# Second layer: another plan of ticks for the routing, and a token gather by digits of 64 and 20

## The chip, the cores and the metric

The kernel runs on one core of a Trainium2 chip. The metric is the device time of one execution in microseconds. The median of three runs before the change is 1599.07 us (1598.33 to 1605.1).

## The reference

The program has three parts: a spectral mixing of x (4 x 2496 tokens of 256 features), a mixture-of-experts layer with the best expert for each token, and a second such layer in which each of the eight experts takes at most N/8 = 1248 tokens. Only the second layer is touched:

```python
cap = N // E
logits = x @ w_gate
order = np.argsort(-logits.flatten())
assigned = -np.ones(N, dtype=np.int64)
counts = np.zeros(E, dtype=np.int64)
for idx in order:
    tok, e = int(idx) // E, int(idx) % E
    if assigned[tok] >= 0 or counts[e] >= cap:
        continue
    assigned[tok] = e
    counts[e] += 1
for e in range(E):
    mask = assigned == e
    h = np.maximum(x[mask] @ w1[e], 0.0)
    out[mask] = h @ w2[e]
```

## The kernel before

`Route2` replaces the greedy loop by eight phases. A phase finds the expert that fills up next, the tokens that it takes, and a list of their rows; `Moe2` then computes that expert on 1248 tokens in three blocks (384, 384 and 480; in the last phase 512, 384 and 352). The 9984 tokens and the padding of the first layer lie in 128 partitions x 92 columns (`NCOL`).

In a phase five passes search a threshold. Each compares all values with 16 bounds (`cmp`, in two halves, VectorE, tile `q_cmp`), counts by expert (`count`, 12 bf16 matmuls that load `q_cmp` as weights and stream 64 columns of `q_oh`), takes the diagonal (`diag`, tiles `q_dx`, `q_dd`), sums it (`total`, two matmuls) and narrows the bounds (`narrow`, tiles `q_nr`, `q_nn`, `q_th`). Then `pick` and `above` find the full expert and the tokens over its threshold, `left` and `number` update what room is left (`q_f`, `q_qi`), `before` is a prefix count over the partitions in f32 (`q_s`), `close` shuts the expert in the logits (`l<-l,q_pe`), `best0` to `best3` find the best open expert of every token (`q_vr`, `q_g`, `q_fi`, `q_oh`), and `take` marks the tokens (`q_tk`, `q_free`).

For the list, `members` ranks the tokens of the expert and `digits` (`q_base`, `q_ri`, `q_lo`, `q_hb`) splits a rank into a high digit (10 values) and a low digit (128 values). `high` makes a one-hot `q_hh` of the high digit, once times the column number (VectorE) and once times the partition number (ScalarE). `low(i)` makes the one-hot `q_lu` of the low digit for a quarter of 23 columns: 128 x 23 elements, the column index innermost. `gather(i)` runs 23 matmuls for a quarter: the weights are the 128 low-digit columns of one token column (a stride of 23 elements), and 2 x 10 columns of `q_hh` are streamed. The result is 128 x 20 for each quarter, in one PSUM bank (`q_bank`). `index` adds the four quarters and makes the row numbers (`q_ix`), by which GpSimd gathers the tokens from memory with indirect DMAs (tile `y`).

In `Moe2` a block's tokens are transposed (`yt`, TensorE), split into two parts (`yh` by ScalarE, `yl` by VectorE), multiplied by w1 (`e<-yh,w1H` and so on, three matmuls for each product), passed through a relu that splits again (`zh` by ScalarE, `zl` by VectorE) and multiplied by w2. Three PSUM buffers serve both the transposes and the first product. The weights are split by ScalarE (`w1H`, `w2H`) and GpSimd (`w1L`, `w2L`).

All instructions of one engine run in the order in which they are issued. The order is a plan of ticks: `tk.at(k, kind, fn)` puts a function at tick k, and in each tick the kinds run in a fixed order, of which these matter here: loads, `pm` (also inside the first product of a tick), `ev` (relu and token splits), `rt` (routing on VectorE), `pe` (gemms and transposes), `ev2` (weight splits), `pd` (rest of the first layer), `pr` (routing on TensorE). The tables `FAST0`, `PACE1`, `PACE` and `FAST` hold the offsets in ticks of each step for phase 0, phase 1, phases 2 to 6 and phase 7. A block has a gemm of the first product every second tick; the first gemm is at tick 26 for phase 0's expert, at 88 for phase 1's, at 138 for phase 2's and 48 ticks later for each further one. The rest of the first layer (six slots, `g<-w2z,z`) fills TensorE in ticks 1 to 17.

Of the kernel before, what the change touches and what calls it, by code (L numbers as in the profile page):

```python
# [24 lines left out]
P = 128  # L25
# [568 lines left out]
class Setup:  # L594
# [35 lines left out]

    def make3(self, nc, cp):
        io = self.misc[:, 0:128]
        self.iota10 = cp.tile([P, NB2, NCOL], BF16, name="iota10")
        nc.scalar.add(
            self.iota10, io[:, 0:NB2].unsqueeze(2).broadcast_to([P, NB2, NCOL]), 1.0
        )
        self.iota = cp.tile([P, P, 23], BF16, name="iota23")
        nc.scalar.add(self.iota, io.unsqueeze(2).broadcast_to([P, P, 23]), 1.0)

    def make(self, nc):  # L640
        misc = self.misc
# [574 lines left out]
class Moe1:  # L1216
# [341 lines left out]
    "gather": (7, 8, 9, 10), "index": 11,  # L1558
}
FAST0 = {  # L1560
    "cmp": 0, "count": 0, "diag": 1, "total": 1, "pass": 2, "pick": 0, "above": 0, "left": 0,
    "number": 0, "sure": 6, "close": 6, "before": 0, "best0": 6, "take": 1, "best1": 6, "best2": 6,
    "best3": 7, "next": 7, "list": 0, "before2": 1, "digits": 2, "high": 2, "low": 2, "step": 1,
    "gather": (2, 3, 4, 5), "index": 6,
}
PACE = {
    "cmp": 1, "count": 3, "diag": 4, "total": 5.5, "pass": 8, "pick": 0, "above": 0, "left": 1,
    "number": 3, "sure": 9, "close": 2, "before": 2.0, "best0": 3, "take": 4, "best1": 5,
    "best2": 5, "best3": 8, "next": 8, "list": 6, "before2": 4, "digits": 5, "high": 10, "low": 14,
    "step": 2.5, "gather": (15, 17, 20, 22), "index": 23,  # L1570
}
PACE1 = {
    "cmp": 0, "count": 3.5, "diag": 4, "total": 5.5, "pass": 6, "pick": 0, "above": 0, "left": 1,
    "number": 2, "sure": 9, "close": 4, "before": 2.5, "best0": 5, "take": 6, "best1": 7,
    "best2": 7, "best3": 8, "next": 10, "list": 6, "before2": 4, "digits": 5, "high": 10, "low": 13,
    "step": 2.5, "gather": (15, 17, 20, 22), "index": 23,
}
LEAD = {
    "y": 11, "yt": 7, "relu": 2, "g2": 9, "st": 18, "w1l": 24, "w2l": 12, "w1": 19, "w1s": 3,
# [11 lines left out]
class Route2:  # L1591
# [11 lines left out]
    def __init__(self, tc, S, l2, valid, cp, ep):  # L1603
        self.tc, self.S, self.l2, self.valid = tc, S, l2, valid
        t = lambda shape, nm, dt=F32: cp.tile(shape, dt, name=nm)
        self.free = t([P, NCOL], "q_free")
        self.asn = t([P, NCOL], "q_asn")
        self.kk = t([P, E], "q_kk")
        self.l0 = t([P, 1], "q_l0")
        self.bad = t([P, 1], "q_bad")  # L1610
        self.l2c = t([P, E, NCOL], "q_l2c")
        self.lo = self.hi = None
        self.exact = False
        self.turn = {}
# [4 lines left out]
        self.vr, self.g, self.fn, self.on = self.own  # L1619

    def open(self, tmp, pp):
        self.tmp = tmp
# [33 lines left out]
    PLACES = {"cnt": (0, 64), "tot": (128, 128), "bf": (384, 2)}  # L1656
    ACC = 388

    def ps(self, nm, shape):

# [54 lines left out]
    def close(self, pe):  # L1715
        self.tc.eng.vector.tensor_tensor(
            self.l2, self.l2, pe.unsqueeze(2).broadcast_to([P, E, NCOL]), ALU.add
        )

    def best(self, n, s=None):  # L1720

        vec = self.tc.eng.vector
        sh = [P, E, NCOL]
        new = s is None
        if new:
            s = slice(0, NCOL)
# [12 lines left out]
        if n == 0:  # L1739
            vec.tensor_reduce(vr, self.l2[:, :, s].rearrange("p e c -> p c e"), AX.X, ALU.max)  # L1740
        elif n == 1:
            vec.tensor_tensor(
                g, self.l2[:, :, s], vr.unsqueeze(1).broadcast_to(sh), ALU.is_ge
            )
        elif n == 2:
            vec.tensor_tensor(g, g, self.S.w8b[:, :, s], ALU.mult)
            vec.tensor_reduce(fn, g.rearrange("p e c -> p c e"), AX.X, ALU.max)
        else:
            vec.tensor_tensor(on, g, fn.unsqueeze(1).broadcast_to(sh), ALU.is_equal)

# [12 lines left out]
    def phase(self, tk, k, ph, soon):  # L1763
# [233 lines left out]
        def digits():  # L1997
            base = T([P, 1], "q_base")
            vec.tensor_scalar_add(base, st["p"], -1.0)
            ri = T([P, NCOL], "q_ri", I32)  # L2000
            vec.tensor_scalar(ri, st["s"], base, None, ALU.add)
            hi = T([P, NCOL], "q_hi2", I32)
            li = T([P, NCOL], "q_li", I32)
            vec.tensor_single_scalar(li, ri, P - 1, ALU.bitwise_and)
            vec.tensor_single_scalar(hi, ri, 7, ALU.arith_shift_right)
            lo = T([P, NCOL], "q_lo", BF16)
            vec.scalar_tensor_tensor(lo, li, 1.0, st["m"], ALU.add, ALU.mult)
            hb = T([P, NCOL], "q_hb", BF16)
            vec.tensor_scalar_add(hb, hi, 1.0)
            st["lo"], st["hb"] = lo, hb  # L2010

        def high():
            hh = self.late.tile([P, 2, NB2, NCOL], BF16, name=f"q_hh{self.n}", tag="q_hh", bufs=1)
            sh = [P, NB2, NCOL]
            vec.tensor_tensor(
                hh[:, 0], st["hb"].unsqueeze(1).broadcast_to(sh), S.iota10, ALU.is_equal
            )
            vec.tensor_tensor(
                hh[:, 1], hh[:, 0], S.colv.unsqueeze(1).broadcast_to(sh), ALU.mult
            )  # L2020
            nc.scalar.mul(hh[:, 0], hh[:, 0], S.pv)
            st["hh"] = hh

        def low(i):
            self.uniq()
            u = self.late.tile([P, P, 23], BF16, name=f"q_lu{self.n}", tag="q_lu", bufs=4)
            vec.tensor_tensor(
                u,
                S.iota,
                st["lo"][:, 23 * i : 23 * i + 23].unsqueeze(1).broadcast_to([P, P, 23]),  # L2030
                ALU.is_equal,
            )
            st["u", i] = u

        def gather(i):

            o = self.ACC + 2 * NB2 * i
            u = st.pop(("u", i))
            for c in range(23):
                nc.tensor.matmul(  # L2040
                    self.bank[:, o : o + 2 * NB2],
                    u[:, :, c],
                    st["hh"][:, :, :, 23 * i + c].rearrange("p v b -> p (v b)"),
                    start=c == 0,
                    stop=c == 22,
                )

        def index():
            a = T([P, 2, NB2], "q_ia")
            vec.tensor_reduce(  # L2050
                a.rearrange("p v b -> p (v b)"),
                self.bank[:, self.ACC : self.ACC + 8 * NB2].rearrange("p (i x) -> p x i", i=4),
                AX.X,
                ALU.add,
            )
            f = T([P, NB2], "q_if")
# [10 lines left out]
        def pe(t, fn):  # L2067
            tk.at(int(t), "pm" if t % 1 else "pr", fn)
# [8 lines left out]
        else:  # L2077
            for i in range(passes):
                f = FAST if k < soon else c
                tk.at(k, "rt", lambda: cmp(0))  # L2080
                tk.at(k + f["cmp"], "rt", lambda: cmp(1))
                pe(k + f["count"], count)
                tk.at(k + f["diag"], "rt", diag)
                pe(k + f["total"], total)
                k += f["pass"]
                tk.at(k, "rt", narrow)
            for nm, f in (
                ("pick", pick),
# [17 lines left out]
        tk.at(k + c["digits"], "rt", digits)  # L2106
        tk.at(k + c["high"], "rt", high)
        for i in range(4):
            tk.at(k + c["low"] + int(c["step"] * i), "rt", lambda i=i: low(i))
            pe(k + c["gather"][i], lambda i=i: gather(i))  # L2110
        tk.at(k + c["index"], "rt", index)
        return kn, kq, k + c["index"] + 1, st

# [328 lines left out]
```

## Time and profile before

| | |
|---|---|
| median of three runs | 1599.07 us (1598.33 to 1605.1) |
| profiled execution | 1602.92 us, of which span 1601.1 us |
| TensorE matmul busy | 1470.2 us (92%) |
| TensorE weight load busy | 1358.2 us (85%) |
| VectorE busy | 1086.1 us (68%) |
| ScalarE busy | 726.7 us (45%) |
| GpSimd busy | 776.3 us (48%) |
| mean granted TensorE clock | 0.959 |

The span runs from the first to the last instruction. Matmuls overlap and their ends are modelled, so a step between two starts is a better cost than the busy time of one. The chain of work that ended last gives 28% of the span to TensorE and 13% to VectorE, most in pieces of some microseconds that alternate between them. The second layer's routing starts at about 911 us; its last index is made at 1470 us.

### The profile page before, as it was taken

The numbers are of one execution on the slowest core, as the hardware profiler recorded it, in microseconds if no ns is written. First come the engines' busy times: TensorE is split into PE (matmuls) and PEld (weight loads), VectorE is DVE, ScalarE is ACT, GpSimd is POOL, SyncE is SP. The second block draws the span as 40 slices with busy tenths as digits, with TensorE's granted clock in tenths as the row PEclk, the third lists the DMA queues.
The fourth block names the chain that finished last, engine by engine and source line by source line (L and its number), as shares of the span: only waits on it lengthen the run. The fifth ranks groups of instructions, "written<-read, shape, count | busy, mean of one in ns | idle before, by whom it ended". The sixth has DMA issues, their size and how long they took to land. (4 is left out here: it accounts for less than half of the span.)

```text
span 1601.1 us, 32607 instructions
## 1 busy us (share of the span) xinstructions
PE 1470.2 (92%) x11619; PEld 1358.2 (85%) x11619; DVE 1086.1 (68%) x2040; ACT 726.7 (45%) x1557; POOL 776.3 (48%) x759
## 2 busy tenths in 40 slices
PE   6899999798899999999999896898989899999997
PEld 3899999567899998898898775887889888889997
DVE  4797768836997666566566676788596868675321
ACT  4355555555566656566666422222232323233332
POOL 2342323116777776777776204263444444455542
PEclk8899999989999999999999997999999999999999
DMA  7766754763111551221221242212021212122111
GB/s 236 243 211 204 230 158 130 245 197 116 34 38 50 141 145 44 69 60 50 66 59 47 89 122 83 77 36 83 27 92 31 89 31 88 31 82 81 59 43 35
DMA packets 128623, 158.30 MB, mean 99 GB/s; under 512 B 31163, under 2 KB 108206, under 8 KB 128445
## 3 DMA queue, kind: packets, MB, share of 16 engines
q1 hardware_dynamic: 99837, 102.42, 21.1%
q0 software_dynamic: 15744, 36.23, 7.5%
q10 hardware_dynamic: 12864, 17.41, 3.3%
q8 instruction: 96, 1.57, 0.4%
q14 instruction: 82, 0.67, 0.1%
HBM read 170.69 MB, written 53.30 MB: 140 GB/s over the span
## 5 line engine op out<-in xcount | busy, mean ns | idle before, releaser
L145 DVE TENSOR_TENSOR w1l<-w1r,w1h 128x512 fp32r<-128x512 f32 x168 | 209.3, 1246 | 83.5 <-ACT w1h L145 70.1
L145 PE MATMUL g<-w2h,hl 128*128 128x264 f32 x1152 | 240.7, 290 | 8.6 <-DVE hl L145 8.2
L145 POOL TENSOR_TENSOR w2l<-w2r,w2h 128x528 fp32r<-128x528 f32 x144 | 197.9, 1393 | 96.9 <-ACT w2h L145 36.5
L145 ACT ACTIVATE zh<-e 128x384 fp32r<-128x384 f32 (+3 forms) x192 | 99.4, 518 | 317.2 <-PE e L145 302.2
L145 DVE SCALAR_TENSOR_TENSOR zl<-e,zh 128x384 fp32r<-128x384 f32 (+3 forms) x192 | 112.4, 586 | 129.7 <-ACT zh L145 110.0
L145 PEld LDWEIGHTS g<-w2h,hl 128*128 128x128 f32 x1152 | 188.9, 189 | 11.2 <-DVE hl L145 10.6
L145 PE MATMUL g<-mh,w1h 128*128 128x256 f32 x672 | 193.5, 288 | 2.8 <-issue 2.8
L145 PE MATMUL g<-ml,w1h 128*128 128x256 f32 x672 | 191.9, 286 | 4.2 <-issue 3.9
L145 PE MATMUL g<-mh,w1l 128*128 128x256 f32 x672 | 191.8, 285 | 3.2 <-issue 3.2
L145 PE MATMUL e<-w2H,zh 128*128 128x256 f32 (+1 forms) x640 | 187.3, 293 | 0.0
L145 PE MATMUL e<-w2H,zl 128*128 128x256 f32 (+1 forms) x640 | 182.3, 285 | 0.0
L145 PE MATMUL e<-w2L,zh 128*128 128x256 f32 (+1 forms) x640 | 182.0, 284 | 0.0
L145 PE MATMUL g<-w2l,hl 128*128 128x264 f32 x576 | 164.5, 286 | 0.0
L145 POOL DMA_INDIRECT out_dram<-o,yi x80 | 86.8, 1085 | 154.8 <-ACT o L145 139.6
L145 PE MATMUL e<-yh,w1H 128*128 128x384 f32 (+3 forms) x384 | 146.2, 381 | 14.0 <-DVE zl L145 8.0
L145 PE MATMUL e<-yl,w1H 128*128 128x384 f32 (+3 forms) x384 | 138.4, 360 | 0.0
L145 PE MATMUL e<-yh,w1L 128*128 128x384 f32 (+3 forms) x384 | 138.3, 360 | 0.0
L145 PEld LDWEIGHTS g<-mh,w1h 128*128 128x128 f32 x672 | 130.4, 194 | 9.0 <-issue 5.7
L145 PEld LDWEIGHTS g<-ml,w1h 128*128 128x128 f32 x672 | 130.2, 194 | 5.8 <-issue 5.0
L145 PEld LDWEIGHTS g<-mh,w1l 128*128 128x128 f32 x672 | 130.3, 194 | 4.5 <-issue 4.5
L145 ACT CAST w2h<-w2r 128x528 fp32r<-128x528 f32 x144 | 93.1, 646 | 84.7 <-PE g L145 43.4
L145 PEld LDWEIGHTS e<-w2H,zh 128*128 128x128 f32 (+1 forms) x640 | 122.4, 191 | 1.5
(1219 smaller groups left out, 3941.9 us busy)
## 6 DMA issues: line engine op xcount, KB each, us to landing
w1r<-in_moe_w_dram SPq DMA_DIRECT2D x168, 256.0 KB
w2r<-in_moe_w_dram SPq DMA_DIRECT2D x144, 256.0 KB
x_d<-row ACTq DMA_DIRECT2D x36, 257.0 KB
a<-a_d SPq DMA_DIRECT2D x36, 256.0 KB
w2x<-in_moe_w_dram SPq DMA_DIRECT2D x16, 512.0 KB
w1s<-in_moe_w_dram SPq DMA_DIRECT2D x32, 256.0 KB
w2s<-in_moe_w_dram SPq DMA_DIRECT2D x32, 256.0 KB
xt<-in_x_dram SPq DMA_DIRECT2D x16, 468.0 KB
```

The costliest lines, as they stand in the source:

```text
L145: r = f(*args, **kw)
```

## The change

The gather is turned: the low digit has 64 values and the high digit 20. `low(i)` writes 23 x 64 with the digit innermost, so that a token column's 64 values are contiguous. `high` makes two tiles of 20 x 92, and eight short steps `turn(i, v)` on ScalarE copy them quarter by quarter to 23 x 2 x 20, the first of them scaled by the partition number. In `gather(i)` the 40 high-digit columns are the weights and the 64 low-digit columns are streamed; the result is 40 x 64 for each quarter. `gathered` adds the quarters, two f32 matmuls (`turned`) turn the sum back to 128 x 20, and `index` reads that from PSUM. The large iota of 128 x 23 becomes 64 values.

The two reductions over the eight experts (`best0`, `best2`) become trees of three maxima. The tables change: in `PACE` `close` and `best0` come two ticks later, `best1` one, `best2` two, `digits` three, `index` one; a new entry `wait` puts the first pass's count later, and in phase 1 it puts off a pass that falls within three ticks of the first gemm's tick less three. `index` of phase 0 comes one tick later, and so does its first gemm (tick 27); the later ones keep their ticks (88, 138, ...). Phases 2 to 6 start one tick earlier.

```diff
 PACE = {
-    "cmp": 1, "count": 3, "diag": 4, "total": 5.5, "pass": 8, "pick": 0, "above": 0, "left": 1,
-    "number": 3, "sure": 9, "close": 2, "before": 2.0, "best0": 3, "take": 4, "best1": 5,
-    "best2": 5, "best3": 8, "next": 8, "list": 6, "before2": 4, "digits": 5, "high": 10, "low": 14,
-    "step": 2.5, "gather": (15, 17, 20, 22), "index": 23,
+    "wait": 1, "cmp": 1, "count": 3, "diag": 4, "total": 5.5, "pass": 8, "pick": 0, "above": 0, "left": 1,
+    "number": 3, "sure": 9, "close": 4, "before": 2.0, "best0": 5, "take": 4, "best1": 6,
+    "best2": 7, "best3": 8, "next": 8, "list": 6, "before2": 4, "digits": 8, "high": 10, "low": 14,
+    "step": 2.5, "gather": (15, 17, 20, 22), "index": 24,
 }
...
+    def tree(self, o, x, dt):
+        n = x.shape[2]
+        for h in (4, 2, 1):
+            y = o.unsqueeze(1)
+            if h > 1:
+                y = self.half[dt, h][:, :, :n]
+            self.tc.eng.vector.tensor_tensor(y, x[:, 0:h], x[:, h : 2 * h], ALU.max)
+            x = y
...
+        def turn(i, v):
+            if v == 0:
+                st["hh", i] = self.late.tile(
+                    [P, 23, 2, NH], BF16, name=f"q_hh{self.n}_{i}", tag=f"q_hh{i}", bufs=1
+                )
+            o = st["hh", i][:, :, v]
+            x = st["hx"][v][:, :, 23 * i : 23 * i + 23].rearrange("p b c -> p c b")
+            if v == 0:
+                nc.scalar.mul(o, x, S.pv)
+            else:
+                nc.scalar.copy(o, x)
...
         def low(i):
             self.uniq()
-            u = self.late.tile([P, P, 23], BF16, name=f"q_lu{self.n}", tag="q_lu", bufs=4)
+            sh = [P, 23, HALF]
+            u = self.late.tile(sh, BF16, name=f"q_lu{self.n}", tag="q_lu", bufs=4)
             vec.tensor_tensor(
                 u,
-                S.iota,
-                st["lo"][:, 23 * i : 23 * i + 23].unsqueeze(1).broadcast_to([P, P, 23]),
+                S.iotal.unsqueeze(1).broadcast_to(sh),
+                st["lo"][:, 23 * i : 23 * i + 23].unsqueeze(2).broadcast_to(sh),
                 ALU.is_equal,
             )
...
                 nc.tensor.matmul(
-                    self.bank[:, o : o + 2 * NB2],
-                    u[:, :, c],
-                    st["hh"][:, :, :, 23 * i + c].rearrange("p v b -> p (v b)"),
+                    self.bank[: 2 * NH, o : o + HALF],
+                    hh[:, c].rearrange("p v b -> p (v b)"),
+                    u[:, c],
                     start=c == 0,
                     stop=c == 22,
                 )
...
+        def gathered():
+            a = st["a"] = T([2 * NH, HALF], "q_ga")
             vec.tensor_reduce(
...
+        def turned():
+            for h in range(2):
+                nc.tensor.matmul(
+                    self.bank[HALF * h : HALF * h + HALF, self.IDX : self.IDX + NH],
+                    st["a"],
+                    S.ident[: 2 * NH, h : 2 * NH : 2],
+                    start=True,
+                    stop=True,
+                )
...
             for i in range(passes):
                 f = FAST if k < soon else c
-                tk.at(k, "rt", lambda: cmp(0))
+                o = f["wait"] if "wait" in f and (i == 0 or 0 < soon <= k < soon + 3) else 0
+                late = o if f is PACE1 else 0
+                tk.at(k + late, "rt", lambda: cmp(0))
+                tk.at(k + late + f["cmp"], "rt", lambda: cmp(1))
+                pe(k + o + f["count"], count)
...
-            tk.at(k + c["low"] + int(c["step"] * i), "rt", lambda i=i: low(i))
+            t = k + c["low"] + int(c["step"] * i)
+            tk.at(t, "rt", lambda i=i: low(i))
+            for v in range(2):
+                tk.at(max(t - 1 + v, k + c["high"]), "ev2", lambda i=i, v=v: turn(i, v))
             pe(k + c["gather"][i], lambda i=i: gather(i))
+        tk.at(k + c["index"] - 1, "rt", gathered)
+        pe(k + c["index"] - 1, turned)
         tk.at(k + c["index"], "rt", index)
```

## Rows read from the trace of the kernel before

**Rows 1.** Busy time by stretch: TensorE, weight load, VectorE, ScalarE, GpSimd; clock, DMA.

```profile
960.00:990.00 30.00, 17.05 (x135) 13.89 (x133) 18.92 (x41) 4.61 (x10) 10.11 (x11) 0.67 0.34 101
...
1213.00:1292.00 79.00, 73.25 (x575) 67.43 (x574) 60.20 (x145) 23.73 (x53) 36.88 (x39) 0.98 0.19 61
...
1470.00:1601.00 131.00, 121.33 (x859) 117.24 (x857) 35.62 (x70) 43.57 (x100) 56.93 (x69) 0.98 0.15 48
```

**Rows 2.** TensorE's waits from 990 to 1475 us: in total, times, longest.

```profile
PE e L145 <- DVE zl L145: 8.0, 11, 2.1
PE yt L145 <- DVE zl L145: 5.6, 3, 3.9
...
PE e L145 <- DVE q_free L145: 3.6, 2, 1.9
PE q_bank L145 <- DVE q_base L145: 3.4, 2, 1.8
...
PE yt L145 <- DVE q_f L145: 1.4, 3, 0.5
```

**Rows 3.** TensorE in order of time, 1258 to 1278 us: start, duration, instruction.

```profile
1258.20 0.28 PE L145 MATMUL q_bank<-q_s,misc 128*128 128x1 f32 x2
...
1271.71 0.73 PE L145 MATMUL q_bank<-q_oh,q_cmp 128*128 128x64 bf16 x12
1272.28 0.36 PE L145 MATMUL e<-w2H,zh 128*128 128x256 f32 x1
...
1272.71 0.28 PE L145 MATMUL e<-w2H,zh 128*128 128x256 f32 x1
1272.83 0.28 PE L145 MATMUL e<-w2L,zh 128*128 128x256 f32 x1
...
1275.93 1.64 PE L145 MATMUL q_bank<-q_hh,q_lu 128*128 128x20 bf16 x23
1277.42 0.37 PE L145 MATMUL e<-w2H,zh 128*128 128x256 f32 x1
```

**Rows 4.** Weight loads by form: count, busy us, mean ns, idle before.

```profile
L145 PEld LDWEIGHTS <-q_cmp 128*128 128x128 bf16 x385 | 18.3, 102 | 23.5 <-DVE q_cmp L145 10.6 <-issue 7.2 <-DVE q_w L145 3.3
...
L145 PEld LDWEIGHTS <-q_cmp 128*64 128x64 bf16 x35 | 3.8, 109 | 2.0
```

**Rows 5.** VectorE's groups by form.

```profile
L145 DVE TENSOR_TENSOR q_lu<-iota,q_lo 128x2944 bf16<-128x2944 bf16 x32 | 61.0, 1913 | 0.0
...
L145 DVE TENSOR_REDUCE q_vr<-l 128x92 f32<-128x736 f32 x7 | 11.0, 1567 | 0.0
L145 DVE TENSOR_REDUCE q_fi<-q_g 128x92 bf16<-128x736 bf16 x7 | 10.2, 1452 | 0.2
...
L145 DVE TENSOR_TENSOR f_hh<-f_hh,v 117x1540 bf16<-117x1540 bf16 x4 | 7.0, 1749 | 0.0
...
L145 DVE TENSOR_TENSOR l<-l,q_pe 128x736 f32<-128x736 f32 x7 | 6.4, 916 | 0.0
L145 DVE TENSOR_TENSOR q_hh<-q_hh,colv 128x920 bf16<-128x920 bf16 x8 | 5.1, 637 | 0.3
...
L145 DVE TENSOR_TENSOR q_g<-q_g,w8b 128x736 bf16<-128x736 bf16 x7 | 3.8, 542 | 0.2
```

**Rows 6.** VectorE in order of time, `narrow` to `above` of phase 4, first and last.

```profile
1240.36 0.28 DVE L145 TENSOR_REDUCE q_nr<-q_bank 128x16 f32<-128x128 f32 x1
...
1244.94 0.35 DVE L145 TENSOR_TENSOR_SCAN q_s<-ones,q_bi 128x92 f32<-128x92 bf16 x1
```

**Rows 7.** TensorE and VectorE in order of time, 978 to 988 us.

```profile
978.65 0.66 PE L145 MATMUL yt<-ident,y 128*128 128x128 f32 x2 [2.60 <-DMA y<-x_d,q_ix]
...
984.22 2.89 DVE L145 TENSOR_TENSOR q_cmp<-q_v,q_th 128x768 bf16<-128x768 f32 x2
...
987.71 0.67 PE L145 MATMUL e<-yh,w1H 128*128 128x384 f32 x1
```

**Rows 8.** ScalarE's scaling of the one-hot, by form.

```profile
L145 ACT ACTIVATE q_hh<-q_hh,misc 128x920 bf16<-128x920 bf16 x8 | 8.5, 1062 | 15.3 <-DVE q_hh L145 13.6 <-issue 1.7
```

More of the change, by code (lines that the diff above doesn't have):

```diff
@@ L41 @@
 NB2 = 10
+HALF = 64
+NH = 20
 CLOSED = 30000.0
@@ L632, in make3 @@
         io = self.misc[:, 0:128]
[L633 to L638, printed above, removed]
+        self.iotah = cp.tile([P, NH, NCOL], BF16, name="iotah")
+        nc.scalar.add(self.iotah, io[:, 0:NH].unsqueeze(2).broadcast_to([P, NH, NCOL]), 1.0)
+        self.iotal = cp.tile([P, HALF], BF16, name="iotal")
+        nc.scalar.copy(self.iotal, io[:, 1 : 1 + HALF])
     def make(self, nc):
@@ L1557 @@
     "best3": 1, "next": 2, "list": 1, "before2": 2, "digits": 3, "high": 6, "low": 6, "step": 1,
-    "gather": (7, 8, 9, 10), "index": 11,
+    "gather": (7, 8, 9, 10), "index": 12,
 }
@@ L1563 @@
     "best3": 7, "next": 7, "list": 0, "before2": 1, "digits": 2, "high": 2, "low": 2, "step": 1,
-    "gather": (2, 3, 4, 5), "index": 6,
+    "gather": (2, 3, 4, 5), "index": 7,
 }
 PACE = {
-    "cmp": 1, "count": 3, "diag": 4, "total": 5.5, "pass": 8, "pick": 0, "above": 0, "left": 1,
-    "number": 3, "sure": 9, "close": 2, "before": 2.0, "best0": 3, "take": 4, "best1": 5,
-    "best2": 5, "best3": 8, "next": 8, "list": 6, "before2": 4, "digits": 5, "high": 10, "low": 14,
-    "step": 2.5, "gather": (15, 17, 20, 22), "index": 23,
+    "wait": 1, "cmp": 1, "count": 3, "diag": 4, "total": 5.5, "pass": 8, "pick": 0, "above": 0, "left": 1,
+    "number": 3, "sure": 9, "close": 4, "before": 2.0, "best0": 5, "take": 4, "best1": 6,
+    "best2": 7, "best3": 8, "next": 8, "list": 6, "before2": 4, "digits": 8, "high": 10, "low": 14,
+    "step": 2.5, "gather": (15, 17, 20, 22), "index": 24,
 }
 PACE1 = {
-    "cmp": 0, "count": 3.5, "diag": 4, "total": 5.5, "pass": 6, "pick": 0, "above": 0, "left": 1,
+    "wait": 2, "cmp": 0, "count": 3.5, "diag": 4, "total": 5.5, "pass": 6, "pick": 0, "above": 0, "left": 1,
     "number": 2, "sure": 9, "close": 4, "before": 2.5, "best0": 5, "take": 6, "best1": 7,
     "best2": 7, "best3": 8, "next": 10, "list": 6, "before2": 4, "digits": 5, "high": 10, "low": 13,
-    "step": 2.5, "gather": (15, 17, 20, 22), "index": 23,
+    "step": 2.5, "gather": (15, 17, 20, 22), "index": 24,
 }
@@ L1619, in __init__ @@
         self.vr, self.g, self.fn, self.on = self.own
+        self.half = {
+            (d, h): t([P, h, NCOL], f"e_m{i}{h}", d) for i, d in enumerate((F32, BF16)) for h in (4, 2)
+        }
     def open(self, tmp, pp):
@@ L1654, in t @@
         return self.tmp.tile(shape, dt, name=nm + str(self.n), tag=nm, bufs=bufs)
-    PLACES = {"cnt": (0, 64), "tot": (128, 128), "bf": (384, 2)}
-    ACC = 388
+    PLACES = {"cnt": (0, 0), "tot": (64, 0), "bf": (192, 2)}
+    IDX = 196
+    ACC = 216
     def ps(self, nm, shape):
@@ L1739, in best @@
         if n == 0:
-            vec.tensor_reduce(vr, self.l2[:, :, s].rearrange("p e c -> p c e"), AX.X, ALU.max)
+            self.tree(vr, self.l2[:, :, s], F32)
         elif n == 1:
@@ L1746, in best @@
             vec.tensor_tensor(g, g, self.S.w8b[:, :, s], ALU.mult)
-            vec.tensor_reduce(fn, g.rearrange("p e c -> p c e"), AX.X, ALU.max)
+            self.tree(fn, g, BF16)
         else:
@@ L2003, in digits @@
             li = T([P, NCOL], "q_li", I32)
-            vec.tensor_single_scalar(li, ri, P - 1, ALU.bitwise_and)
-            vec.tensor_single_scalar(hi, ri, 7, ALU.arith_shift_right)
+            vec.tensor_single_scalar(li, ri, HALF - 1, ALU.bitwise_and)
+            vec.tensor_single_scalar(hi, ri, 6, ALU.arith_shift_right)
             lo = T([P, NCOL], "q_lo", BF16)
@@ L2012, in high @@
         def high():
[L2013 to L2016, printed above, removed]
-            )
[L2018 to L2022, printed above, removed]
+            sh = [P, NH, NCOL]
+            e, x = (
+                self.late.tile(sh, BF16, name=f"q_h{c}{self.n}", tag=f"q_h{c}", bufs=1) for c in "ex"
+            )
+            vec.tensor_tensor(e, st["hb"].unsqueeze(1).broadcast_to(sh), S.iotah, ALU.is_equal)
+            vec.tensor_tensor(x, e, S.colv.unsqueeze(1).broadcast_to(sh), ALU.mult)
+            st["hx"] = e, x
+        def turn(i, v):
[9 more added lines that the diff above has]
+                nc.scalar.copy(o, x)
         def low(i):
             self.uniq()
-            u = self.late.tile([P, P, 23], BF16, name=f"q_lu{self.n}", tag="q_lu", bufs=4)
+            sh = [P, 23, HALF]
+            u = self.late.tile(sh, BF16, name=f"q_lu{self.n}", tag="q_lu", bufs=4)
             vec.tensor_tensor(
                 u,
-                S.iota,
-                st["lo"][:, 23 * i : 23 * i + 23].unsqueeze(1).broadcast_to([P, P, 23]),
+                S.iotal.unsqueeze(1).broadcast_to(sh),
+                st["lo"][:, 23 * i : 23 * i + 23].unsqueeze(2).broadcast_to(sh),
                 ALU.is_equal,
@@ L2035, in gather @@
         def gather(i):
-            o = self.ACC + 2 * NB2 * i
-            u = st.pop(("u", i))
+            o = self.ACC + HALF * i
+            u, hh = st.pop(("u", i)), st.pop(("hh", i))
             for c in range(23):
                 nc.tensor.matmul(
-                    self.bank[:, o : o + 2 * NB2],
-                    u[:, :, c],
-                    st["hh"][:, :, :, 23 * i + c].rearrange("p v b -> p (v b)"),
+                    self.bank[: 2 * NH, o : o + HALF],
+                    hh[:, c].rearrange("p v b -> p (v b)"),
+                    u[:, c],
                     start=c == 0,
@@ L2046, in gather @@
                 )
-        def index():
-            a = T([P, 2, NB2], "q_ia")
+        def gathered():
+            a = st["a"] = T([2 * NH, HALF], "q_ga")
             vec.tensor_reduce(
-                a.rearrange("p v b -> p (v b)"),
-                self.bank[:, self.ACC : self.ACC + 8 * NB2].rearrange("p (i x) -> p x i", i=4),
+                a,
+                self.bank[: 2 * NH, self.ACC : self.ACC + 4 * HALF].rearrange(
+                    "p (i x) -> p x i", i=4
+                ),
                 AX.X,
@@ L2055, in index @@
             )
+        def turned():
[7 more added lines that the diff above has]
+                )
+        def index():
+            a = self.bank[:, self.IDX : self.IDX + NH].rearrange("p (v b) -> p v b", v=2)
             f = T([P, NB2], "q_if")
@@ L2079, in phase @@
                 f = FAST if k < soon else c
-                tk.at(k, "rt", lambda: cmp(0))
[L2081 to L2085, printed above, removed]
+                o = f["wait"] if "wait" in f and (i == 0 or 0 < soon <= k < soon + 3) else 0
[3 more added lines that the diff above has]
+                pe(k + o + f["count"], count)
+                tk.at(k + o + f["diag"], "rt", diag)
+                pe(k + o + f["total"], total)
+                k += f["pass"] + late
                 tk.at(k, "rt", narrow)
```

## The prediction

> **What bounds the kernel now.** I read the busy shares by stretch first, then the waits of TensorE, then single rows of the engines. In the table by stretch [rows 1] the last 640 us are the second layer. From 1470 us on TensorE alone sets the time: nothing of the routing is left there and it is busy for 121.3 of 131 us, the rest being the gaps that its modelled ends leave and the close of the program. In a steady phase (1213 to 1292) it is busy 73.3 of 79 us, VectorE 60.2 and ScalarE 23.7, so TensorE is the bound there too, with some 6 us of waits. From 960 to 990 it is the other way round: TensorE is busy 17 of 30 us at a granted clock of 0.67, because the first tokens of the layer wait for the routing. The list of TensorE's waits from 990 to 1475 us [rows 2] names VectorE on every line; its 13 lines add up to 38 us, of which the five shown here make 22. So three things can shorten the layer: less TensorE work for the routing, fewer of these 38 us, and a shorter passage at 970 to 988.
>
> **TensorE: the gather.** Each of eight phases has 4 quarters of 23 matmuls. Today one loads 128 strided columns of `q_lu` and streams 20. A quarter begins at 1275.93 and the next work at 1277.42: 1.49 us, 65 ns a pair [rows 3]. Afterwards a pair loads 40 contiguous columns and streams 64. The nearest row is the count, which loads contiguous columns and also streams 64: 12 pairs from 1271.71 to 1272.28, 47.5 ns each [rows 3]. Bounds: 65 ns above (nothing won), and below 30 ns, because 256 streamed columns step by 0.12 us (1272.71 to 1272.83), so 64 of them need 30 [rows 3]. I take 47.5, being nearest in shape: 92 x 17.5 ns = 1.6 us less in a phase. New are the two turning matmuls in f32. One f32 matmul of the prefix count is recorded as two passes of together 0.28 us [rows 3], so two cost 0.56 at most; half of that where their start-up overlaps other work. I take 0.4. Net 1.2 us a phase, and over phases 1 to 7, where TensorE is the bound, **8 us** less (between 3 more and 20 less). Phase 0's share lies in the passage below.
>
> The line by form of the weight loads shows 102 ns for 128 columns of `q_cmp` and 109 ns for its last group of 64 [rows 4]: fewer columns are no shorter load. The Trainium skill ("TensorE: Matmul & The Clock Gate", section "Weight-path perf modes — Fast Weight Load (FWL) and DoubleRow") says that the fast load is on only with 128 weights that are not fp32, at four columns a cycle. That speaks against this part: 40 columns would fall out of it, and load in 40 cycles instead of 32. By its figures that is an estimate of 3 ns a pair, 2 us over seven phases, and the 8 us above would be 6 (the total 1584 instead of 1582). The 64-column row agrees with it in sign.
>
> **VectorE: about the same work.** `low` falls from 2944 to 1472 elements, which looks like half. But its second operand is now one value held over 64 elements. The row that has such an operand, all bf16, is `f_hh<-f_hh,v`: 1540 elements in 1749 ns, whereas `q_lu` does 2944 in 1913 on average [rows 5]. With 736 f32 elements in 916 ns the slope is 1.04 ns an element and the fixed part 153 [rows 5]; so the new `low` costs 1.68 us, four of them 0.9 us less than today. Were it as fast an element as today it would be 1.0 us each, 3.8 us less; that is the other bound. I take 1.68. `high` doubles to 1840 elements twice: from 542 ns at 736 and 637 at 920 [rows 5] the slope is 0.52, so 1.11 us each, 0.95 us more in all. `gathered` reads 256 elements instead of 80, some 0.2 more. The tree in place of the first reduce (1567 ns) is three f32 steps of 368, 184 and 92 elements, 0.54 + 0.34 + 0.25 = 1.13; in place of the second (1452) three bf16 steps, 0.35 + 0.26 + 0.21 = 0.82 [rows 5]. That is 1.1 us less. Sum: 0.9 us less in a phase of 60; 3.7 less with the other bound of `low`, 0.6 less if the bf16 steps run no faster than f32. The amount hardly matters; where it stands does.
>
> **The plan of ticks.** A phase is 48 ticks of 1.65 us. Today `close`, `best0`, `take`, `best1`, `best2`, `members`, the next phase's `first` and its comparisons, and `digits` all sit in ticks 99 to 108 (phase 2), just where a new block's `yl` and `zl` have to pass the same queue. The four large ones shown alone are 4.5 us there (0.92 + 1.57 + 0.54 + 1.45) [rows 5], and they come right behind `narrow`, `pick` and `above`, some 18 instructions in tick 97; in phase 4 they run from 1240.36 to 1245.29, 4.9 us or three ticks [rows 6]. VectorE arrives late in tick 99, and TensorE waits. The waits that carry names from this run are `q_free` 3.6, `q_base` 3.4 and `q_f` 1.4 us [rows 2], and those on `zl` (8.0 and 5.6) partly. Afterwards `close` and `best0` come two ticks later, `best1` apart from `best2`, and `digits` stands at 110, behind the first count; the first comparisons have three ticks instead of two before their count. What goes: `q_base` and `q_f` wholly and most of `q_free`, 7 us, and a third of the 13.6 on `zl`, 4.5. What is late next: `pick` and `above` still are one block of 4.9 us in one tick [rows 6], so the long wait for `zl` behind them (up to 3.9 us) and the `q_s` waits stay. And because VectorE has the same work, some of it moves: `high` at tick 112 now stands for 2.2 us in front of `narrow`. I take **9 us** (0 to 18).
>
> **The passage at 970 to 988.** Today the second pass of phase 1 (`narrow`, both comparisons) is put where the first three token tiles arrive. The transpose starts at 978.65; the comparisons run from 984.22 for 2.89 us, slowed by GpSimd's splits; only behind them come two `yl` and the count, and the first gemm at 987.71 [rows 7]. Afterwards this pass is at ticks 23 and 24 with gemm1 at 27, and the third pass waits until 28. So `narrow` and the comparisons run in the idle 4 us before 979. Against that the index is late by `gathered` and the turn: about 0.8 us, less the 4 x 0.4 us that the quarters win. Count 1 and its total now stand between the transposes on TensorE (about 2 us at the low clock). I get gemm1 at about 985: **3 us** (0 to 5).
>
> **What it adds in waits.** The turn waits on TensorE for `gathered`; queued behind it are the next gemms. One tick lies between the last quarter and it, `gathered` takes 0.4, so 0.3 us a phase, 2 us (0 to 6). On ScalarE eight turns a phase replace one scaling of 920 elements, 1062 ns [rows 8]. A turn has 460: between 0.53 and 1.06, I take 0.65 us, 5.2 in all, 4 more than now. ScalarE is busy 24 of 79 us [rows 1], which hides them; they come one or two a tick. Behind a turn stand `zh` and the weight splits, hence 1 us for late `zh`. The iota for 23 columns also goes from ScalarE, in tick 5, while TensorE works off the first layer's rest: nothing, and nothing if that cover were gone but the copy's own length, once.
>
> **Sum.** 8 + 9 + 3 - 2 - 1 = 17 us. The profiled execution took 1602.9 us (span 1601.1 and 1.8 around it), so it would take 1585.9. The median of the runs is 1599.1, 3.8 below it. Predicted: **1582 us**.
>
> **Rivals.**
> 1. *The waits only move and the gather is no faster.* For it: VectorE's work is the same to 1 us in 60, and every wait is on VectorE. Against it: `close` to `digits` is visibly the dense place. Then 3 us of the passage and a few of the waits are left, less the turn: 1595.
> 2. *More goes than I take.* The gather at 30 ns (20 us), nearly all waits of this stretch (18), the passage (4): some 40 us, 1560. For it: nothing but these rows' bounds; against it, `pick` and `above` are untouched.
> 3. *ScalarE holds up TensorE: slower.* A turn stands in front of `zh` and waits for `high` or for its place; with three PSUM buffers shared by gemm1 and the transposes a late `zh` stops gemm1. It decides once `zh` is later than the two or so ticks that the buffers give. Price, if each turn shows fully: 8 x 0.65 x 7 = 36 us, less the 20 gained: 1615. Against it: ScalarE's low share and the turns' spread; for it: in the first and last phase three turns share the tick of `high`.
> 4. *It doesn't do what it says in one part:* `low` is not cheaper. That is already my forecast; were it to halve, 3 us of VectorE a phase, of which TensorE would see the waits on `q_lu`, 3 us in all: 1579.
>
> **Chances.** Forecast (with 4) 0.58, own range 1574 to 1590; rival 1 0.19; rival 2 0.12; rival 3 0.11. About 0.5% (8 us) is what a measurement of this kernel can tell from no change. Under 1591: nearly all of the forecast, rival 2 and a quarter of rival 1, 0.72. Within: most of rival 1 and a little of the rest, 0.17. Slower: rival 3, 0.11. The range reaches from halfway to rival 2, 1567, to just past rival 1, 1599.
>
> **What would show it.** Right: gathers of 23 pairs in about 1.1 us; `q_lu` at 1.7 us in spite of half the elements; the waits on `q_base` and `q_f` gone; the first gemm of the layer 3 us earlier; the stretch after the last index as long as before. Wrong: gathers still at 1.5 us; new waits of TensorE on `q_hh`, `q_ga` or on `zh` by ScalarE; a steady phase still 79 us long.

## The result, and the profile after

The changed kernel takes **1580.1 us** (median of 6 runs, 1574.8 to 1582.8), the kernel before 1597.7 us (6 runs, 1594.0 to 1605.1): ratio 0.9888, 95% interval 0.9862 to 0.9914, some 18 us. The forecast was 1582. The profiled execution took 1574.8 us (span 1572.8). In it the second layer, from its first transpose (`e_am`) to the end of the span, lasts 665.0 us (907.8 to 1572.8); before it was 684.8 (916.3 to 1601.1): 19.8 us. The first layer's code is the same and its time moves by several us from run to run, so below the second layer stands beside each ratio. Each such time comes from one profiled execution, and here that execution is the shortest of the six.

The table by stretch of the changed kernel: the start of the layer, one steady phase, the part after the last index; its columns are those of [rows 1].

```profile
950.00:980.00 30.00, 20.31 (x169) 15.97 (x167) 23.35 (x57) 10.07 (x19) 12.44 (x13) 0.72 0.35 101
1195.60:1271.20 75.60, 68.82 (x575) 63.42 (x574) 60.04 (x147) 30.14 (x60) 34.58 (x38) 1.00 0.20 63
1442.00:1572.80 130.80, 120.99 (x854) 116.63 (x852) 35.40 (x70) 43.61 (x100) 56.95 (x69) 0.97 0.15 48
```

A steady phase falls from 79.0 to 75.6 us, TensorE in it from 73.3 to 68.8, at a clock of 1.00 instead of 0.98; VectorE keeps its 60 us. The last part is as long as before.

TensorE's waits of the changed kernel, 974 to 1447 us (in total, times, longest), against [rows 2]:

```profile
PE e L147 <- DVE zl L147: 9.9, 5, 3.1
PE yt L147 <- DVE zl L147: 6.0, 2, 3.1
PE q_bank L147 <- DVE q_cmp L147: 5.4, 9, 1.2
PE q_bank L147 <- DVE q_dd L147: 5.4, 8, 1.9
PE q_bank L147 <- DVE q_s L147: 5.3, 2, 3.6
PE q_bank L147 <- DVE q_dx L147: 4.2, 8, 0.7
PE q_bank L147 <- DVE q_bi L147: 3.3, 3, 1.1
...
PE q_bank L147 <- DVE q_lu L147: 0.6, 3, 0.2
PE q_bank L147 <- DVE q_ga L147: 0.5, 1, 0.5
```

`q_free`, `q_base` and `q_f` are gone, as forecast. Yet the sum is not smaller (45 us, before 38): TensorE arrives earlier and waits for other results of the same VectorE, which ends 42.6 of the 45 us.

One quarter of the gather on TensorE, the answer to [rows 3], and the first gemm of the layer, which answers to [rows 7]:

```profile
948.04 0.83 PE L147 MATMUL q_bank<-q_lu,q_hh 128*40 128x64 bf16 x23
948.80 0.92 PE L147 MATMUL g<-w2z,z 128*128 128x256 f32 x3
...
968.99 1.76 DVE L147 TENSOR_TENSOR q_cmp<-q_v,q_th 128x768 bf16<-128x768 f32 x2
...
974.46 0.69 PE L147 MATMUL e<-yh,w1H 128*128 128x384 f32 x1 [0.46 <-ACT yh L147]
```

A quarter takes 0.76 us from start to next start, 33 ns a pair instead of 65. The comparisons of the second pass take 1.76 us instead of 2.89, and the first gemm comes 66.7 us after the layer's first transpose (974.5 - 907.8) instead of 71.4.

VectorE and ScalarE by form (busy us, mean ns, idle before), against [rows 5] and [rows 8]:

```profile
L147 DVE TENSOR_TENSOR q_lu<-iotal,q_lo 128x1472 bf16<-128x1472 bf16 x32 | 54.1, 1698 | 0.0
L147 DVE TENSOR_TENSOR q_he<-q_hb,iotah 128x1840 bf16<-128x1840 bf16 x8 | 8.9, 1118 | 0.2 <-DVE q_hb L147 0.2
...
L147 DVE TENSOR_TENSOR e_m<-l 128x368 f32<-128x368 f32 x7 | 3.7, 531 | 0.0
...
L147 DVE TENSOR_TENSOR q_vr<-e_m 128x92 f32<-128x92 f32 x7 | 3.7, 527 | 0.2
L147 DVE TENSOR_TENSOR e_m<-e_m 128x184 f32<-128x184 f32 x7 | 3.5, 502 | 0.2
L147 DVE TENSOR_REDUCE q_ga<-q_bank 40x64 f32<-40x256 f32 x8 | 3.3, 417 | 9.2 <-PE q_bank L147 9.2
...
L147 ACT ACTIVATE q_hh<-q_he,misc 128x460 bf16<-128x460 bf16 x32 | 36.2, 1130 | 4.6 <-POOL rowz L147 3.1 <-issue 1.5
L147 ACT COPY q_hh<-q_hx 128x460 bf16<-128x460 bf16 x32 | 32.5, 1016 | 0.0
```

### The profile page after: what moved, and what is told of

Same layout as the page of the kernel before. It is cut to its first block, busy times and chain, and to the rows that moved or that the text cites. A ratio compares the mean times of both kernels' runs of the same rounds, so it can differ in the third digit from the quotient of the medians.

```text
span 1572.8 us, 32766 instructions
## 1 busy us (share of the span) xinstructions
PE 1445.6 (92%) x11651; PEld 1330.5 (85%) x11651; DVE 1091.1 (69%) x2076; ACT 778.6 (50%) x1613; POOL 771.1 (49%) x759
## 3 DMA queue, kind: packets, MB, share of 16 engines
q8 instruction: 96, 1.57, 0.4%
## 5 line engine op out<-in xcount | busy, mean ns | idle before, releaser
L147 DVE TENSOR_TENSOR w1l<-w1r,w1h 128x512 fp32r<-128x512 f32 x168 | 216.1, 1287 | 70.9 <-ACT w1h L147 53.7
L147 PE MATMUL g<-mh,w1h 128*128 128x256 f32 x672 | 189.9, 283 | 3.5 <-issue 3.3
L147 PE MATMUL g<-mh,w1l 128*128 128x256 f32 x672 | 188.3, 280 | 1.0 <-issue 1.0
L147 PE MATMUL e<-yh,w1H 128*128 128x384 f32 (+3 forms) x384 | 145.1, 378 | 10.3 <-DVE zl L147 9.9
L147 PEld LDWEIGHTS g<-mh,w1h 128*128 128x128 f32 x672 | 127.1, 189 | 9.6 <-issue 7.1
L147 ACT CAST w2h<-w2r 128x528 fp32r<-128x528 f32 x144 | 93.1, 647 | 75.6 <-PE g L147 48.3
L147 PEld LDWEIGHTS g<-ml,w1h 128*128 128x128 f32 x672 | 127.0, 189 | 4.2 <-issue 3.5
L147 PEld LDWEIGHTS g<-mh,w1l 128*128 128x128 f32 x672 | 126.9, 189 | 3.0 <-issue 3.0
```

The source lines that it names most:

```text
L147: r = f(*args, **kw)
```

## The experiments

The kernel before ran beside the others each time, so ratios are to it. The edits below are shown in short. "Two phases" is the time between two indices two steady phases apart, with TensorE's busy time, the sum of its waits and the mean clock in it.

| run | ratio, 95% | second layer | two phases | busy | waits | clock |
|---|---|---|---|---|---|---|
| before | 1 | 684.8 | 157.9 | 147.6 | 10.3 | 0.97 |
| e1 changed kernel | 0.9882 (0.985 to 0.9913) | 664.1 | 151.2 | 137.6 | 13.7 | 1.00 |
| e2 old gather | 0.992 (0.989 to 0.9951) | 670.1 | 153.1 | 143.0 | 10.1 | 0.99 |
| e3 old plan | 0.9981 (0.996 to 1.0001) | 681.0 | 159.7 | 142.2 | 17.5 | 0.97 |
| e4 old reductions | 0.9885 (0.9853 to 0.9917) | 665.2 | | | | |
| e5 low in pairs | 0.9812 (0.9793 to 0.983) | 655.0 | 147.9 | 138.6 | 9.2 | 0.99 |
| e6 high written directly | 0.9881 (0.9862 to 0.99) | 659.8 | | | | |
| e7 above a tick later | 0.9868 (0.9845 to 0.9891) | 665.5 | | | | |
| e9 spread undone | 0.9963 (0.9941 to 0.9986) | 678.1 | 159.6 | 142.1 | 17.5 | 0.97 |
| e10 waiting ticks undone | 0.9907 (0.9879 to 0.9934) | 668.3 | 153.6 | 139.3 | 14.4 | 0.99 |
| e11 e5 and e6 together | 0.9807 (0.9779 to 0.9835) | 653.5 | 147.9 | 138.6 | 9.3 | 0.99 |
| e12 old plan, low in pairs | 0.9936 (0.9914 to 0.9957) | 670.2 | 152.6 | 139.5 | 13.1 | 0.99 |

The two phases lie early in the layer. The same quantities from the second index of the layer to the last, in which every steady phase lies and the passage at its start doesn't:

| run | time | busy | waits | clock |
|---|---|---|---|---|
| before | 408.4 | 376.5 | 31.9 | 0.96 |
| e1 changed kernel | 391.3 | 354.8 | 36.5 | 0.98 |
| e2 old gather | 397.0 | 367.0 | 30.0 | 0.98 |
| e5 low in pairs | 386.7 | 356.4 | 30.3 | 0.97 |
| e9 spread undone | 407.4 | 362.4 | 45.0 | 0.96 |

**One part undone at a time (e1 to e4).**

> The changed kernel itself, as the level for the three runs beside it. Both theories: 1580 us, about 17 below the kernel before.

Changed kernel again: 1552.6 us against 1572.4, on a chip on which both are shorter; the ratio agrees.

```diff
 e2: make3, PLACES, digits, high, low, gather, index as before; turn, gathered and turned left out
 e3: PACE and PACE1 as before, but  "index": 23  ->  "index": 24  (the turn needs the tick)
     and  g - LEAD0["soon"]  ->  g - LEAD0["soon"] - 1  (the later blocks then come a tick later too)
 e4: -            self.tree(vr, self.l2[:, :, s], F32)
     +            vec.tensor_reduce(vr, self.l2[:, :, s].rearrange("p e c -> p c e"), AX.X, ALU.max)
     (and the same for fn)
```

> The changed kernel with the gather of before (digits of 128 and 10, 128 strided weight columns, no turns), new plan and trees kept; its index still in the new tick. Theory G (the gather's TensorE time is the gain): a pair goes from 33 to 65 ns, 92 pairs and eight phases less the turning matmuls, 20 us slower than the changed kernel, 1598 or a little less. Theory P (the plan of ticks gives half of it, as predicted): 8 slower, 1588.

> The changed kernel with the tables of before for phases 1 to 6 (close, best0 to best2, digits in their old ticks, no wait), all one tick later because the index needs a tick more; new gather and trees kept. Theory P: 9 us of waits and 3 to 4 of the passage come back, 1592. Theory G: only the passage, 4 us, 1584.

> The changed kernel with the two reductions of before in place of the trees: 1.1 us more of VectorE in each of seven phases. If VectorE's length in that stretch goes to TensorE one to one: 7 us slower, 1587. If it lies beside TensorE's work: 1580.

Undoing the gather costs 6.0 us of the second layer, undoing the plan 16.9, the trees 1.1, which can't be told from nothing. Theory P holds for the larger share, and more than it expected; theory G falls. The old gather has 5.4 us more of TensorE in two phases and 3.6 fewer waits; from the second index to the last 12.2 more and 6.5 fewer: more than half of what the fast gather saves comes back as waiting. Taken from the other side, the plan with the trees (e2) is worth 0.8%, 12.6 us, and the gather with the trees (e3) 0.2%, with an interval that still holds 1: without the plan the faster gather buys next to nothing. Two things keep these prices rough. In e3 every later block comes one tick of 1.65 us later than in the changed kernel, and that may be part of its 16.9. And e2 also gives the counts their second place in the PSUM bank back (`PLACES`), which no run takes by itself.

**VectorE's load, ScalarE's turns, the block of pick and above (e5 to e7).**

```diff
 e5: lo holds each value twice, [P, NCOL, 2], and low compares with it in pairs
-  lo[:, 23i:23i+23].unsqueeze(2).broadcast_to([P, 23, HALF])
+  lo[:, 23i:23i+23].unsqueeze(2).broadcast_to([P, 23, HALF // 2, 2])
 e6: VectorE writes the high one-hot as [P, NCOL, 2, NH] (in pairs too); ScalarE only scales, in place
 e7: -"above": 0   +"above": 1   in PACE and PACE1
```

> The changed kernel, with the low digit kept twice beside itself, so that the innermost step of every operand of the comparison is 1 again. A comparison of 1472 elements should go from 1.68 to 0.95 us, 2.9 us less of VectorE in a phase. Theory V (VectorE's load in the stretch of the lows holds TensorE back, and ate most of what the gather saved): 8 to 15 us faster than the changed kernel, second layer 650 to 657 us instead of 665. Theory B (the wait is one block of VectorE, pick and above, and the load elsewhere has cover): within 2 us of it.

> The changed kernel with the high one-hot written by VectorE straight into the layout of the weights (pairs, so that the innermost step is 1), and only four scalings by ScalarE: the eight turns of 1.0 to 1.1 us in a phase become four of about 0.7. If ScalarE's turns hold up zh and so TensorE (rival 3 of the prediction, in a small form): 3 to 10 us faster. If ScalarE's share has cover: within 2 us of the changed kernel.

> The changed kernel with above one tick behind pick in phases 1 to 6, so that zl and yl can pass between the two parts of the block of 4.9 us. Theory B: the waits for zl behind the block (4.3 us in two phases) and the drop of the granted clock that follows a long one go: 6 to 12 us faster. Theory V: 2 us or less.

Theory V holds in its number, the rest falls. In e5 `low` costs 0.92 us in the median (mean 995 ns), as VectorE's row by form shows:

```profile
L147 DVE TENSOR_TENSOR q_lu<-iotal,q_lo 128x1472 bf16<-128x1472 bf16 x32 | 31.6, 995 | 0.0
```

VectorE is busy 111.6 us in two phases instead of 120.2, TensorE's waits fall from 13.7 to 9.2, and the time by 0.7% against the changed kernel. The waits that went, first of e1, then of e5 (`q_dx` and `q_lu` end none there any more), each with the table line of its two phases:

```profile
PE q_bank L147 <- DVE q_dx L147: 2.5, 4, 0.7
...
PE q_bank L147 <- DVE q_dd L147: 2.1, 4, 0.7
PE q_bank L147 <- DVE q_lu L147: 0.4, 2, 0.2
```

```profile
1175.50:1326.70 151.20, 137.58 (x1149) 126.72 (x1148) 120.16 (x294) 60.45 (x120) 69.99 (x76) 1.00 0.20 63
```

```profile
PE q_bank L147 <- DVE q_dd L147: 0.6, 2, 0.3
```

```profile
1190.60:1338.50 147.90, 138.60 (x1149) 127.69 (x1148) 111.55 (x294) 60.49 (x120) 69.09 (x76) 0.99 0.20 65
```

So TensorE does wait on the time that VectorE takes, not only on its places. That this time is `low`'s own is shown in part only: of the 8.6 us, `low` gives 4.8. Another 4.3 are `q_cmp` (13.2 to 11.0) and `q_dd` (5.1 to 3.0), which have the same work as before but run beside a weight split of GpSimd less often; such a meeting stretches them by about 1 us. From the second index to the last `low` gives 16.4 of 21.0. No run parts the two. With four of the eight turns gone and the other four shorter (e6), and with `above` a tick later (e7), the ratios stay within the interval of the changed kernel's.

**The price of a gather pair (e8).** Seven extra groups of 23 matmuls behind the last index, all else as in the changed kernel; n is the number of columns loaded, `near` says whether they are adjacent.

```diff
+  for n, near, cols in (128, no, 20), (128, yes, 20), (128, no, 64), (128, yes, 64),
+                       (40, no, 64), (40, yes, 64), (40, yes, 20):
+      v = pw as "(c n) -> n c" if near else "(n c) -> n c"      # c: 23
+      23 x matmul(bank[:n, :cols], v[:, :, c], pm[:, :cols])
```

> The changed kernel with seven groups of 23 bf16 matmuls added among the last gemms, on a constant tile: weights of 128 or 40 columns, strided by 23 or contiguous, and 20 or 64 streamed columns; its time is longer by their sum, some 8 us. If the stride makes the pair dear: 128 contiguous and 20 streamed about 35 ns, 128 strided 65, 40 strided with 64 streamed more than 33. If the count of weight columns does: 128 contiguous near 60 as well, and 40 strided near 33.

TensorE in order of time: each group in the order of the list, and the work that starts next.

```profile
1463.89 1.65 PE L147 MATMUL q_bank<-pm,pw 128*128 128x20 bf16 x23
1465.40 0.42 PE L147 MATMUL e<-yh,w1H 128*128 128x384 f32 x1
...
1470.79 0.74 PE L147 MATMUL q_bank<-pm,pw 128*128 128x20 bf16 x23
1471.38 0.37 PE L147 MATMUL e<-w2H,zh 128*128 128x256 f32 x1
...
1476.99 1.64 PE L147 MATMUL q_bank<-pm,pw 128*128 128x64 bf16 x23
1478.46 0.42 PE L147 MATMUL e<-yh,w1H 128*128 128x384 f32 x1
...
1484.48 0.85 PE L147 MATMUL q_bank<-pm,pw 128*128 128x64 bf16 x23
1485.16 0.36 PE L147 MATMUL e<-w2H,zh 128*128 128x256 f32 x1
...
1491.16 1.90 PE L147 MATMUL q_bank<-pm,pw 128*40 128x64 bf16 x23
1492.98 0.49 PE L147 MATMUL e<-yh,w1H 128*128 128x480 f32 x1
...
1499.25 0.85 PE L147 MATMUL q_bank<-pm,pw 128*40 128x64 bf16 x23
1500.03 0.39 PE L147 MATMUL e<-w2H,zh 128*128 128x256 f32 x1
...
1508.16 0.74 PE L147 MATMUL q_bank<-pm,pw 128*40 128x20 bf16 x23
1508.83 0.49 PE L147 MATMUL e<-yh,w1H 128*128 128x480 f32 x1
```

From start to next start, divided by 23: 128 columns 66 ns strided and 26 adjacent (20 streamed), 64 and 30 (64 streamed); 40 columns 79 strided, 34 adjacent, and 29 with 20 streamed. The stride is the price: 34 to 45 ns. With adjacent columns their number hardly counts (40 cost 3 to 4 ns more than 128); strided, 40 cost 15 ns more than 128. There is one group of each kind. The one run lasted 1586.1 us; its second layer is 5.9 us longer than the changed kernel's.

**The two halves of the plan (e9, e10).**

```diff
 e9: PACE  -"close": 4, "best0": 5, "best1": 6, "best2": 7, "digits": 8
           +"close": 2, "best0": 3, "best1": 5, "best2": 5, "digits": 5
 e10: PACE -"wait": 1    PACE1 -"wait": 2
```

> The changed kernel with one half of its plan undone: in the steady table close, best0, best1, best2 and digits stand at their old ticks again (2, 3, 5, 5, 5); the extra tick of waiting before the first counts and the later third pass stay. Undoing the whole plan cost 16.9 us in the second layer (681.0 instead of 664.1 us from its first transpose to the end). Theory S, the dense place is what holds TensorE: this half alone costs 10 to 14 us, the second layer 675 to 679, ratio to before 0.995 to 0.998. Theory W, the tick of waiting before the counts does it: 2 to 5 us, 667 to 670, ratio 0.990 to 0.992.

> The other half undone: the spread stays, the extra ticks before the first counts are gone (both tables), and with them the earlier second pass of phase 1. Theory S: only the passage of the prediction (4.7 us as measured) and little of the steady phases come back, 4 to 7 us in all, second layer 669 to 672, first gemm of the layer again about 71 us after its start instead of 67. Theory W: 10 to 14 us, second layer 675 to 679, with waits on q_base in every phase. If either half alone gives all of the 17 us back, the halves only work together.

Undoing the spread costs 14.0 us of the second layer, undoing the waiting ticks 4.2; together 18, about the 16.9 of both at once. Theory S holds. The sum is rough: e9 leaves the later blocks in their ticks, but e10 brings them two ticks forward, as e3 brings them one tick back, so the 4.2 may be net of up to 3 us. How the dense place costs time stands in these rows. First e9, VectorE and TensorE in order of time, in brackets the idle time and what ended it:

```profile
1214.55 0.92 DVE L147 TENSOR_TENSOR q_g<-l,q_vr 128x736 bf16<-128x736 f32 x1
1215.49 1.49 DVE L147 TENSOR_TENSOR q_g<-q_g,w8b 128x736 bf16<-128x736 bf16 x1
...
1217.81 0.55 DVE L147 SCALAR_TENSOR_TENSOR zl<-e,zh 128x384 fp32r<-128x384 f32 x1
...
1213.24 0.44 PE L147 MATMUL yt<-ident,y 128*128 128x128 f32 x2 [0.77 <-DVE zl L147]
...
1218.42 0.69 PE L147 MATMUL e<-yh,w1H 128*128 128x384 f32 x1 [3.29 <-DVE zl L147]
```

and its table by stretch behind that wait:

```profile
1218.40:1221.40 3.00, 2.98 (x11) 2.98 (x12) 1.83 (x7) 0.49 (x1) 2.23 (x3) 0.51 0.99 337
1221.40:1224.40 3.00, 3.00 (x23) 3.00 (x23) 2.93 (x12) 0.49 (x1) 0.62 (x1) 1.00 0.49 135
```

Then the same place in the changed kernel:

```profile
1230.23 1.21 DVE L147 TENSOR_TENSOR q_vr<-e_m 128x92 f32<-128x92 f32 x1
1231.37 0.55 DVE L147 SCALAR_TENSOR_TENSOR zl<-e,zh 128x384 fp32r<-128x384 f32 x1
...
1231.96 0.44 PE L147 MATMUL e<-yh,w1H 128*128 128x384 f32 x1 [2.10 <-DVE zl L147]
```

```profile
1232.00:1235.00 3.00, 3.00 (x20) 3.00 (x21) 2.86 (x9) 0.49 (x1) 2.39 (x3) 1.00 1.09 347
```

In e9 `best1` and `best2` run as one block and `zl` stands behind them (1217.81). TensorE waits 3.29 us, and then runs for 3 us at a granted 0.51, the lower of its two levels (1.2 of 2.4 GHz): another 1.5 us (3.0 x 0.49). In the changed kernel the two are apart, `zl` has only `best0` in front of it, TensorE waits 2.10 us and the clock stays at 1.00. In two phases the old places cost 8.4 us: 3.8 of waits and 4.5 of busy time at the lower clock; from the second index to the last 16.1: 8.5 and 7.6. About 1 us of each of the two waits is a stretched instruction: the second instruction of e9's block takes 1.49 us instead of the usual 0.53, and the last step of `best0`'s tree 1.21 instead of 0.25, each beside a weight split of GpSimd.

**Load and plan together (e11, e12).** e11 is e5 with e6; e12 is e3 with e5.

> The changed kernel with both changes to the one-hots: low compares in pairs (about 0.92 instead of 1.68 us each), and VectorE writes the high one-hot in the order in which TensorE loads it, with the four turns of column numbers on ScalarE gone. If VectorE's load is still what TensorE waits for, the gains add: second layer 655 less some 4 = 651, ratio to before 0.976 to 0.980. If the pairs already took what was to be had: 655 and 0.981, the same as with the pairs alone.

> The plan of ticks as before, with the new gather and low compared in pairs. Theory L, plan and load cure the same lateness of VectorE: with a phase 3 us lighter on VectorE the old plan loses little, second layer 657 to 662 and ratio 0.985 or less. Theory D, the old places are wrong whatever the load: the plan still costs its 17 us, second layer 670 to 673, ratio 0.990 to 0.993.

e11 is not told apart from e5 by its ratio; it is, with e5, the fastest version here, 1.9% below the kernel before. In e12 the old plan still costs 15.2 us (670.2 against 655.0), so theory D holds: plan and load are two separate faults, and their gains add. (e12 has the later tick of e3; it may make up to 1.65 us of the 15.2.)

## Why the prediction was right, step by step

- **Total: right.** Some 18 us measured, 17 forecast; but its largest terms came about otherwise than the sum has them, as the next points show.
- **Plan and passage: right size, the path only half.** 9 + 3 us forecast; the plan with the trees and without the new gather (e2) gives 12.6 us, with an interval from 8 to 17. The named waits went, but the sum of all waits hardly fell: between the second index and the last, from the kernel before to e2, 1.9 us of 11.4 are fewer waits and 9.5 are TensorE doing the same matmuls in less time, at 0.98 instead of 0.96. What the sum lacked is this clock, so its 9 us met the size by another path than the one that it gave, which is luck. With the new gather the plan is worth more, about half of it through the clock (e9). The wait that matters most is the `zl` behind `best1` and `best2`, of which the prediction gave back a third only.
- **Passage: size nearly right, cause not.** The first gemm comes 4.7 us earlier in the profile (3 forecast). But with the old tables (e3) it also comes 65.2 us after the layer's first transpose, and without the waiting ticks (e10) 66.8. What these runs have in common with the changed kernel is the extra tick of the first index, which puts the first gemm at tick 27 instead of 26 and so leaves the second pass more room; so the gain goes with that tick, and not with the later third pass. No run undoes the tick alone.
- **Gather: mis-sized, and a term was missing.** 47.5 ns a pair was taken, 33 measured. Four quarters save 2.9 us (4 x (1.49 - 0.76)) and the turn takes 0.29, so TensorE gains 2.6 us a phase instead of 1.2, 18 us over seven phases instead of 8. The missing term is that TensorE then waits for VectorE: 3.6 us in two phases (13.7 less 10.1, e1 and e2), 6.5 from the second index to the last, where TensorE is busy 12.2 less. The waits that the sum did name, 2 us on the turn and 1 on late `zh`, came to little: `q_ga` ends 0.5 us in all. Net 6 us (e2), against 8 - 2 - 1 = 5 forecast. The two errors cancelled, which was luck. The count, taken as nearest in shape, was no measure for the pair: its pairs of 128 columns step by 30 ns, and the one group of 64 columns among the twelve costs some 0.26 us; 47.5 is the mean of both. e8 gives 34 ns for the pair's own shape.
- **The fast load.** With adjacent columns, 40 cost 4 ns more than 128 at 64 streamed columns and 3 more at 20 (e8). The Trainium skill ("TensorE: Matmul & The Clock Gate", section "Weight-path perf modes — Fast Weight Load (FWL) and DoubleRow") has the fast load on only with 128 weights; the estimate of 3 ns from it agrees. (Its 32 cycles are the page's theory for fp8 weights; that they hold for bf16 no run shows.) It is small beside the 34 to 45 ns of the stride.
- **ScalarE's turns: the duration was wrong, the cost right.** 1.02 to 1.13 us each instead of 0.65, 8.6 us a phase instead of 5.2; ScalarE is busy 30.1 of 75.6 us and hides them: e6 and e11 take four of the eight away without a change of the ratio that their intervals, 6 to 9 us wide, could show. Rival 3 falls.
- **VectorE: durations right but one, the conclusion wrong.** `low` at 1.70 us (1.68 forecast), `high` 1.12 (1.11), the trees' bf16 steps 0.35, 0.26 and 0.21 as given. The f32 tree was given 1.13 us and took 1.56 on average (0.53, 0.50, 0.53), as much as the reduction that it replaced (1.57), because in some phases its second or third step runs beside a weight split of GpSimd. So VectorE does 0.2 us less a phase instead of 0.9. But "the amount hardly matters" is refuted: rival 4's variant (`low` halved) was priced at 3 us in all, and e5, where it is halved, gives 9 to 11. The waits on `q_lu`, by which it was priced, are only where VectorE's lateness is last seen; it shows under `q_dx` (2.5 us in two phases) and `q_dd` (2.1, in e5 0.6) too.
- **The rest** is as forecast: the last part as long as before; `pick` and `above` still one block, though parting them (e7) gains nothing that can be measured.

What stays open: why the second layer of e6 is 4 us shorter in its profile while its ratio doesn't show it (the profiled execution was the shortest of its five); how much of e5's gain is `low` itself; and which share of the passage's 4.7 us reaches the end.

## What to carry to other kernels

Where one engine feeds the bound one, read the order of its queue at the place where the wait ends: two large instructions apart by a tick were worth more here than a gather twice as fast, and a long wait can be paid twice, by the lower clock behind it. Price a saving on the bound engine only after asking whether its feeder keeps up; the time freed here came back as waits until the feeder's own work was cut. And sum a feeder's lateness over all waits that name it, not over the tile that you mean to make cheaper.

## What the runs showed of the hardware

- The order of the stationary columns in memory sets the price of a short bf16 matmul: 26 ns for 128 adjacent columns and 66 for the same strided (20 streamed); 34 and 79 for 40 (64 streamed). One group of 23 was run of each (e8).
- A comparison in bf16 whose second operand is one value held over the innermost 64 elements takes 1.68 us for 1472 elements; with each value stored twice, so that the innermost two elements are neighbours, 0.92. The Trainium skill ("VectorE: DVE Perf Modes", section "What auto-detection actually checks") has two elements a cycle for 16-bit tensors with step ±1; the runs agree, and show that two neighbours in a row are enough here.
- ScalarE turns 460 bf16 elements from a strided place in 1.02 to 1.13 us, and scales as many in order in 0.68 (e6).
- VectorE instructions with two tensors as sources take about 1 us longer where they run beside a weight split of GpSimd (`w1L`, `w2L`, 1.26 to 1.9 us): `q_cmp` of 704 elements 1.97 instead of 0.88, `q_dd` 1.36 instead of 0.29 (e1), the last step of the f32 tree 1.21 instead of 0.25 (changed kernel), `q_g<-q_g,w8b` 1.49 instead of 0.53 (e9). The reduction over the experts, with one source, takes 1.50 to 1.51 us beside a split and 1.49 to 1.63 without (e4).
- A TensorE wait of 3.29 us was followed by 3 us at 0.51, one of 2.10 us by 1.00. A limit can't be read from that: in the kernel before, one of 2.08 us is followed by a mean of 0.65 over 4 us. In the last 3 us before these three starts TensorE had been busy for 0.0, 0.9 and 0.4 us.

```profile
1331.05 0.44 PE L145 MATMUL e<-yh,w1H 128*128 128x384 f32 x1 [2.08 <-DVE zl L145]
```

```profile
1331.00:1335.00 4.00, 3.95 (x18) 3.96 (x19) 3.93 (x7) 0.49 (x1) 3.08 (x4) 0.65 0.81 261
```
